# Half of the last block's input stage in two seven-product units

## The chip, the cores and the metric

The kernel runs on one core of a Trainium2 chip. Its time is the device time of one execution in microseconds (us). A profile of one execution gives a span, from the first to the last instruction, and the start and duration of nearly every instruction on the engines: PE (TensorE matmuls; PEld is its weight load), DVE (VectorE), ACT (ScalarE), POOL (GpSimd) and SP, which issues most DMAs. The engines work through their own queues in order and wait for each other with semaphores.

## The reference

Attention inside chunks of 64 tokens, then a feed-forward layer with a squared ReLU:

```python
B, H, S, D = q.shape                       # 8, 8, 576, 64
q_c, k_c, v_c = (t.reshape(B, H, S // 64, 64, D) for t in (q, k, v))
attn = softmax(q_c @ k_c^T / sqrt(D))      # per chunk, 64 x 64
x = (attn @ v_c) -> [4608 tokens, 512]     # heads side by side
h = np.maximum(x @ w_in, 0.0)              # w_in 512 x 2048
out = (h * h) @ w_out                      # w_out 2048 x 512, float32
```

## The kernel before

The 4608 tokens are cut into 18 groups of 256, two groups to a block, so there are nine blocks of 512 tokens, numbered 0 to 8. The matmul operands are bf16, sums are fp32 in PSUM. Each block j has two phases, and while they run the kernel places the attention of block j+1 and the loads, casts and transposes of block j+2 between their steps. The place is written out by hand: a counter `slot` rises by one with each step (`yield`) of a phase, and `plan` says which function is issued at which slot. A block's attention is `scores` (matmuls, then an exp on ACT, L385), `values` (matmuls, then a reciprocal and a multiplication by it on DVE, L408 and L409) and a transpose of x by DMA. Block 8 has nothing left to place: no block follows it.

The **input stage** (`ffn_in`) makes gT, the squared ReLU of x @ w_in, with d_ff on the partitions: 16 tiles of 128 rows by 512 tokens, in the order 8 to 15, then 0 to 7. A tile is four matmuls of 512 columns, one for each 128 rows of d_model (L480), into one of four PSUM banks of the pool `ps_ffn`; ACT takes the ReLU into an fp32 tile `rl` (L471, ring of three); DVE squares it into gT (L475), except tiles 10, 14 and 3, which ACT squares (L473).

The **output stage** (`ffn_out`) of blocks 1 to 8 multiplies gT by w_out in seven products of quarters instead of eight (the scheme of Strassen and Winograd). The quarters of gT are a11 and a12 (tokens 0 to 255, tiles 0 to 7 and 8 to 15), a21 and a22 (tokens 256 to 511). Each product is 16 matmuls of 256 columns (L533). They alternate between two accumulators, n and m; DVE makes the operands d5, d2, d1, d6 and d7 from gT (L493, into `w_st`) and combines the results, ACT copies n out twice (L580, L589). The first product needs a22, the second a11, the third d5 = a11 - a12.

In blocks 2 to 6 the q and k of the block after next are cast to bf16 on ACT (`cast_q` L333, `cast_k` L340) in the output stage. Their fp32 tiles `q_sb` and `k_sb` come from the pool `qk` with five buffers for each name. POOL casts the weights in block 0 (L165, L173) and q and k of the first groups up to block 2; after that it does nothing until it issues stores of the last block (L564, L568). PSUM holds the four banks of `ps_ffn` and two tiles of two banks in `ps_att`, used by the attention alone.

The order of instructions on each engine is the order in which the program issues them (`manual_schedule`). `add(engine, ...)` is a helper, so everything it issues has one line (L493).

Of the kernel before, what the change touches and what calls it, by code (L numbers as in the profile page):

```python
# [10 lines left out]
FP32 = mybir.dt.float32  # L11
BF16 = mybir.dt.bfloat16
AF = mybir.ActivationFunctionType
ALU = mybir.AluOpType
# [3 lines left out]
def kernel(  # L18
# [9 lines left out]
    nc = tc.nc  # L28

    B, H, S, D = q.shape  # L30
# [27 lines left out]
    const_pool = ctx.enter_context(tc.tile_pool(name="const", bufs=1))  # L58
    w_pool = ctx.enter_context(tc.tile_pool(name="w", bufs=1))
    wst_pool = ctx.enter_context(tc.tile_pool(name="wst", bufs=5))  # L60
    in_pool = ctx.enter_context(tc.tile_pool(name="qk", bufs=5))
    att_pool = ctx.enter_context(tc.tile_pool(name="att", bufs=3))
    ffn_pool = ctx.enter_context(tc.tile_pool(name="ffn", bufs=1))
    ps_ffn = ctx.enter_context(tc.tile_pool(name="ps_ffn", bufs=4, space=bass.MemoryType.PSUM))
    ps_att = ctx.enter_context(tc.tile_pool(name="ps_att", bufs=2, space=bass.MemoryType.PSUM))

    ctx.enter_context(tc.manual_schedule())

# [18 lines left out]
    qk = {}  # L87
# [299 lines left out]
    def values(g, tiles=(0, 1)):  # L387
        e = state["e", g]
        veb = v_even[g % NV].bitcast(BF16)
        vob = [v_odd[odd_tile[g, c] % NO].bitcast(BF16) for c in range(4)]  # L390
        if 0 in tiles:
            state["x", g] = att_pool.tile([128, 2, n_hp, 2, D], BF16, name="x", bufs=3)
        x = state["x", g]
        for t in tiles:
            ps = ps_att.tile([128, 2, 512], FP32, name="ps_att")
            for hp in range(n_hp):
                for a in range(2):
                    for p in range(2):
                        c = p ^ a
                        vb = vob[2 * t + p] if a else veb[:, t]  # L400
                        nc.tensor.matmul(  # L401
                            out=ps[64 * p:64 * p + 64, a, hp * (D + 1):(hp + 1) * (D + 1)],
                            lhsT=e[64 * c:64 * c + 64, a, hp, t, :],
                            rhs=vb[64 * c:64 * c + 64, hp, 1::2],
                            start=True, stop=True)
            o = ps[:, :, 0:n_hp * (D + 1)].rearrange("p a (h d) -> p a h d", d=D + 1)
            rec = att_pool.tile([128, 2, n_hp], FP32, name="rec", bufs=4)
            nc.vector.reciprocal(out=rec, in_=o[:, :, :, D])  # L408
            nc.vector.tensor_tensor(  # L409
                out=x[:, t].rearrange("p h a d -> p a h d"),  # L410
                in0=o[:, :, :, 0:D],
                in1=rec.to_broadcast([128, 2, n_hp, D]),
                op=ALU.mult)
# [21 lines left out]
    C, CQ, CK, TD = cast_qk, cast_q, cast_k, transpose_qk_dma  # L435
    SC, AV, XT = scores, values, transpose_x

    def TA(g):
        transpose_qk(g, ps_att, ps_att)

# [8 lines left out]

    gTs = {}  # L450
    LATE_STORES = {j: 26 if j == 2 else 20 for j in range(2, len(blocks) - 1)}
    late = []
    FT_ORDER = [*range(n_ft // 2, n_ft), *range(n_ft // 2)]

    def ffn_in(j, parts, begun={}):
        if j not in gTs:
            gTs[j] = ffn_pool.tile([128, n_ft, BT], BF16, name="gT")
        gT, xT = gTs[j], xTs[j]
        for u, (c, n, ft) in enumerate((c, n, ft) for c, n, fts in parts for ft in fts):
            h = begun.get(ft)  # L460
            if h is None:
                h = ps_ffn.tile([128, 512], FP32, name="ps_ffn")
            for dt in range(n_dt // 2 if ft in begun else 0, n_dt):
                ffn_in_step(h, xT, c, n, ft, dt)
            if j < 3:
                if n == 512 or u % 2 == 0:
                    rl_tile = ffn_pool.tile([128, 512], FP32, name="rl", bufs=3).bitcast(BF16)
                rl = rl_tile[:, u % 2 * 512:] if n < 512 else rl_tile
            else:
                rl = ffn_pool.tile([128, 512], FP32, name="rl", bufs=3)  # L470
            nc.scalar.activation(out=rl[:, 0:n], in_=h[:, 0:n], func=AF.Relu)  # L471
            if (n == 512 and ft in SQUARES_ON_ACT) or (n < 512 and ft in (12, 3)):
                nc.scalar.activation(out=gT[:, ft, c:c + n], in_=rl[:, 0:n], func=AF.Square)  # L473
            else:
                nc.vector.tensor_tensor(  # L475
                    out=gT[:, ft, c:c + n], in0=rl[:, 0:n], in1=rl[:, 0:n], op=ALU.mult)
            yield
# [14 lines left out]
    def add(engine, out, in0, in1, op=ALU.add):  # L492
        engine.tensor_tensor(out=out, in0=in0, in1=in1, op=op)  # L493
# [4 lines left out]
    def ffn_out(j):  # L498
# [110 lines left out]
        for ps, cols, t in parts("m"):  # L609
            add(nc.vector, c22[:, cols], ps, s[:, cols])  # L610
            store(nc.gpsimd, c22, 1, HD, t)
        yield from product("n", d7, b21_p_b22, False)
        c11 = o_tile()
        for ps, cols, t in parts("n"):
# [96 lines left out]
    for j, grps in enumerate(blocks):  # L711
        nxt = blocks[j + 1] if j + 1 < len(blocks) else []
        far = blocks[j + 2] if j + 2 < len(blocks) else []
        plan = {}

        def at(slot, f, g):
            plan.setdefault(slot, []).append((f, g))

        if j == 0:
            loads, go_slots = pieces(far), range(17)  # L720
            at(28, sum_quarters(b11_p_b21, b11, b21), None)
            for slot, f in ((24, TA), (27, SC), (29, AV), (31, XT)):
                at(slot, f, nxt[0])
            at(31, TQ, nxt[1])
            at(31, TK, nxt[1])
            at(31, sum_quarters(b11_m_b22, b11, b22, ALU.subtract), None)
            phases = [first_ffn_in, ffn_out_by_ft(0)]
        elif j == 1:
            loads, go_slots = itertools.chain(*map(qk_pieces, far)), range(26, 48)
            for slot, f in ((4, SC), (8, AV), (12, XT)):  # L730
                at(slot, f, grps[1])
            for i, g in enumerate(nxt):
                for slot, f in ((16 + 4 * i, C), (21 + 4 * i, TD), (36 + i, SC), (38 + 2 * i, AV),
                                (41 + 2 * i, XT)):
                    at(slot, f, g)
            for i, g in enumerate(far):
                at(36 + 4 * i, C, g)
                at(42 + 3 * i, TD, g)
            at(2, sum_quarters(b11_p_b12, b11, b12), None)
            at(12, sum_quarters(b12_p_b22, b12, b22), None)  # L740
            at(20, sum_quarters(b21_p_b22, b21, b22), None)
            phases = [ffn_in(1, [(0, 256, FT_ORDER), (256, 256, FT_ORDER)]), ffn_out(1)]
        else:
            loads, go_slots = pieces(far), range(32)
            slots = {SC: (4, 4), AV: (7, 11), XT: (10, 14), C: (18, 22), TD: (20, 24)}
            if j == 3:
                slots.update({SC: (8, 8), AV: (10, 14), XT: (13, 17)})
                go_slots = [*range(6), *range(13, 32)]
            if not is_whole(nxt[0] if nxt else 0):
                slots.update({SC: (7, 7), AV: (9, 13), XT: (12, 16)})  # L750
            if j == 2:
                loads = itertools.chain(*map(v_pieces, nxt), loads)
                slots = {SC: (8, 10), AV: (12, 15), XT: (15, 18), C: (20, 23), TD: (22, 25)}
                go_slots = [*range(16), *range(25, 36)]
            for f in (SC, AV, XT):
                for i, g in enumerate(nxt):
                    at(slots[f][i], f, g)
            if j > 2 and far and is_whole(far[0]):
                for slot, f, i in ((16, CQ, 0), (18, CK, 0), (18, TD, 0), (18, CQ, 1),
                                   (19, CK, 1), (19, TD, 1)):  # L760
                    at(slot, f, far[i])
            else:
                for f in (C, TD):
                    for i, g in enumerate(far):
                        at(slots[f][i], f, g)
            phases = [ffn_in(j, [(0, BT, FT_ORDER)]), ffn_out(j)]
        slot = 0
        for phase in phases:
            for _ in phase:
                if slot in go_slots:  # L770
                    for f in loads:
                        f()
                        break
                for f, g in plan.get(slot, []):
                    f(g)
                while late and slot >= LATE_STORES[j]:
                    late.pop(0)()
                slot += 1
        assert all(x < slot for x in plan), (j, slot, sorted(plan))
        go(loads)  # L780
        while late:
            late.pop(0)()
# [30 lines left out]
```

## Time and profile before

| | us |
|---|---|
| median of 3 runs | 283.25 |
| the runs | 285.18, 283.25, 282.54 |
| the profiled execution, its own time | 281.17 |
| its span | 279.4 |
| granted TensorE clock over the span | 0.997 |
| PE busy / DVE / ACT / POOL | 269.2 / 186.5 / 160.5 / 35.8 |
| block 8, input stage (from 249.84 to 263.65) | 13.81 |
| block 8, output stage, its 112 matmuls | 12.24 |

Times in the views count from the start of the span. A row of the groups has the line, the engine, the operation, output and inputs with their tile names, the shapes, the count, and then the busy time in us, the mean of one instruction in ns, and the idle time ahead of them with what ended it. The chain of waits is the work that ended last, followed back from the last instruction: start, length and line of each piece. A row of the timeline has start, length, engine, line and operation, with neighbours of one kind merged ("x2").

### The profile page before, as it was taken

The page shows a single profiled execution, that of the slowest core. Times are in us where ns is not written, and L with a number is a line of the kernel's source. Part 1 is how long each engine was busy: PE and PEld are TensorE (multiplying, and loading weights), DVE is VectorE, ACT ScalarE, POOL GpSimd, SP SyncE. Part 2 cuts the span into 40 slices and gives each one's busy share as a digit, 9 for nine tenths or more (in the row PEclk, how much of TensorE's full clock was granted, in tenths as well). Part 3 has the DMA queues.
Part 4 walks back from the last instruction along what each step waited for, and adds up shares of the span by engine and source line. Part 5 has one row for each costly group of instructions (what it writes and reads, how often), then busy time and mean ns, then how long its engine had stood idle before and what let it go on. Part 6 is the DMA issues. An engine that isn't in the chain of part 4 may idle for free.

```text
span 279.4 us, 7179 instructions
## 1 busy us (share of the span) xinstructions
PE 269.2 (96%) x2960; PEld 176.2 (63%) x2963; DVE 186.5 (67%) x304; ACT 160.5 (57%) x269; POOL 35.8 (13%) x62
## 2 busy tenths in 40 slices
PE   6789999989999999999999999999999999999994
PEld 4544455878774487448744874487448744874584
DVE  1446414998943595579549954995579649955793
ACT  2537615885348862877197719762877197218710
POOL 2037844240171000000000000000000000000012
PEclk9999999999999999999999999999999999999998
DMA  7999999989999999979999999979699964141003
GB/s 236 220 345 358 364 332 240 326 212 194 255 207 244 238 213 191 258 183 198 218 245 260 187 184 298 191 158 185 196 238 208 212 199 40 39 109 44 0 21 131
DMA packets 144384, 57.09 MB, mean 204 GB/s; under 512 B 110624, under 2 KB 141600, under 8 KB 144352
## 3 DMA queue, kind: packets, MB, share of 16 engines
q1 hardware_dynamic: 143296, 53.62, 83.8%
q0 software_dynamic: 912, 2.88, 2.8%
q8 instruction: 23, 0.38, 0.6%
q10 hardware_dynamic: 144, 0.13, 0.1%
q14 instruction: 9, 0.07, 0.1%
HBM read 36.70 MB, written 9.44 MB: 165 GB/s over the span
## 4 chain that ended last, share of the span: by engine, by line
PE 80%; DVE 6%; SPq 4%; ACT 2%; DMA 2%; issue 2%; POOL 0%; DVEq 0%; ACTq 0%
PE ps_ffn L480 39%; PE ps_ffn L533 32%; PE ps_ffn L626 5%; SPq L236 3%; DMA w_st<-in_moe_w_in_dram 2%; DVE x L409 2%; DVE gT L475 2%; DVE w_st L493 2%; ACT rl L471 2%; PE ps_att L401 2%; PE ps_att L374 1%; ACT e L385 1%; SPq L227 1%; PE ps_att L428 1%; PE ps_att L190 1%
## 5 line engine op out<-in xcount | busy, mean ns | idle before, releaser
L480 PE MATMUL ps_ffn<-xT,w_in_bf 128*128 128x512 bf16 (+1 forms) x640 | 130.0, 358 | 0.7 <-POOL w_in_bf L165 0.7
L475 DVE TENSOR_TENSOR gT<-rl 128x512 bf16<-128x512 f32 (+2 forms) x132 | 74.2, 593 | 61.4 <-ACT rl L471 60.7
L471 ACT ACTIVATE rl<-ps_ffn 128x512 f32<-128x512 f32 (+2 forms) x160 | 85.7, 554 | 26.9 <-PE ps_ffn L480 23.3
L480 PEld LDWEIGHTS <-w_in_bf 128*128 128x128 bf16 x640 | 60.5, 98 | 58.2 <-POOL w_in_bf L165 2.2
L533 PEld LDWEIGHTS <-w_st 128*128 128x128 bf16 x640 | 62.0, 98 | 8.2 <-DVE w_st L493 0.9
L493 DVE TENSOR_TENSOR w_st<-gT 128x2048 bf16<-128x2048 bf16 x40 | 47.3, 1217 | 0.2
L533 PE MATMUL ps_ffn<-w_out_bf,w_st 128*128 128x256 bf16 x384 | 45.1, 273 | 0.1
L533 PE MATMUL ps_ffn<-w_sum,w_st 128*128 128x256 bf16 x256 | 29.6, 273 | 0.0
L616 ACT COPY o_sb<-ps_ffn 128x512 f32<-128x512 f32 (+1 forms) x8 | 4.5, 559 | 40.3 <-PE ps_ffn L533 40.3
L533 PEld LDWEIGHTS <-gT 128*128 128x128 bf16 x256 | 24.8, 98 | 4.4 <-DVE gT L475 0.2
L568 POOL DMA_DIRECT2D out_dram<-o_sb x4 | 2.2, 553 | 186.2 <-DVE o_sb L493 186.2
L409 DVE TENSOR_TENSOR x<-ps_att,rec 128x512 bf16<-128x512 f32 x32 | 22.1, 691 | 1.1
L385 ACT ACTIVATE e<-ps_att 128x1024 bf16<-128x1024 f32 x16 | 15.8, 1022 | 4.8 <-PE ps_att L374 4.8
L473 ACT ACTIVATE gT<-rl 128x512 bf16<-128x512 f32 (+2 forms) x28 | 16.8, 599 | 0.9
L533 PE MATMUL ps_ffn<-w_out_bf,gT 128*128 128x256 bf16 x128 | 15.3, 273 | 0.0
L533 PE MATMUL ps_ffn<-w_sum,gT 128*128 128x256 bf16 x128 | 15.3, 273 | 0.0
L626 PE MATMUL ps_ffn<-w_out_bf,gT 128*128 128x512 bf16 x61 | 14.2, 379 | 0.3 <-issue 0.2
L165 POOL CAST w_in_bf<-w_st 128x1024 bf16<-128x1024 f32 (+1 forms) x9 | 9.0, 1001 | 17.9 <-DMA w_st<-in_moe_w_in_dram 17.9
L340 ACT CAST qkb<-k_sb 128x1024 bf16<-128x1024 f32 x10 | 10.5, 1047 | 1.2 <-DMA k_sb<-in_k_dram 1.2
L333 ACT CAST qkb<-q_sb 128x1024 bf16<-128x1024 f32 x10 | 10.4, 1044 | 0.0
L626 PEld LDWEIGHTS <-gT 128*128 128x128 bf16 x64 | 6.0, 98 | 7.0
L401 PEld LDWEIGHTS <-e 64*64 64x64 bf16 x512 | 5.8, 107 | 6.3 <-DVE x L409 2.1
(63 smaller groups left out, 157.1 us busy)
## 6 DMA issues: line engine op xcount, KB each, us to landing
q_sb<-in_q_dram SPq DMA_DIRECT2D x16, 512.0 KB, 6.2
k_sb<-in_k_dram SPq DMA_DIRECT2D x24, 256.0 KB, 5.8
out_dram<-o_sb SPq DMA_DIRECT2D x20, 256.0 KB, 3.7
w_st<-in_moe_w_in_dram SPq DMA_DIRECT2D x8, 512.0 KB, 6.8
w_st<-in_moe_w_out_dram SPq DMA_DIRECT2D x8, 512.0 KB, 6.1
ve_sb<-in_v_dram SPq DMA_DIRECT2D x28, 128.0 KB, 3.5
vo_sb<-in_v_dram SPq DMA_DIRECT2D x21, 128.0 KB, 3.0
out_dram<-o_sb POOLq DMA_DIRECT2D x9, 256.0 KB, 5.5
```

The costliest lines, as they stand in the source:

```text
L333: copy(out=qkb[:, 0].rearrange("p (i h d) -> p i h d", i=2, h=H), in_=qk[g][0].rearrange("p t h d -> p (t h d)").rearrange("p (h i d) -> p ...
L340: copy(out=state["qkb", g][:, 1], in_=qk[g][1].rearrange("p t h d -> p (t h d)"))
L385: nc.scalar.activation(out=e_out, in_=s_in, func=AF.Exp, scale=scale)
L401: nc.tensor.matmul(out=ps[64 * p:64 * p + 64, a, hp * (D + 1):(hp + 1) * (D + 1)], lhsT=e[64 * c:64 * c + 64, a, hp, t, :], rhs=vb[64 * c: ...
L409: nc.vector.tensor_tensor(out=x[:, t].rearrange("p h a d -> p a h d"), in0=o[:, :, :, 0:D], in1=rec.to_broadcast([128, 2, n_hp, D]), op=AL ...
L471: nc.scalar.activation(out=rl[:, 0:n], in_=h[:, 0:n], func=AF.Relu)
L473: nc.scalar.activation(out=gT[:, ft, c:c + n], in_=rl[:, 0:n], func=AF.Square)
L475: nc.vector.tensor_tensor(out=gT[:, ft, c:c + n], in0=rl[:, 0:n], in1=rl[:, 0:n], op=ALU.mult)
L480: nc.tensor.matmul(out=h[:, 0:n], lhsT=w_in_bf[:, dt, ft * 128:(ft + 1) * 128], rhs=xT[:, c // 128:(c + n) // 128, dt, :], start=(dt == 0) ...
L493: engine.tensor_tensor(out=out, in0=in0, in1=in1, op=op)
L533: nc.tensor.matmul(out=outs[t], lhsT=a[:, i, t * 128:(t + 1) * 128], rhs=b[:, i, :], start=(first and i == 0 and (last or t == 0)), stop=( ...
L626: nc.tensor.matmul(out=o_ps[tt], lhsT=gT[:, ft, tt * 128:(tt + 1) * 128], rhs=w_out_bf[:, ft, :], start=(ft == 0), stop=(ft == n_ft - 1))
```

## The change

It concerns block 8. Of its 16 input tiles, 12 to 15 (unit a) and 4 to 7 (unit b) are made by seven products of quarters each, the same scheme as in the output stage: a quarter is 256 rows of d_ff by 256 of d_model on the weights' side, and 256 of d_model by 256 tokens on the side of x. A product is four matmuls of 256 columns. The other eight tiles are made as before.

For it, POOL makes five differences of weight quarters for each unit, each of 128x512 bf16, in tiles of the pool `qk` (issued at slot 0 of blocks 6 and 7); DVE makes three sums or differences of x in block 7's output stage, behind the sixth product (`x_sums`); the PSUM of `ps_att` is given to four single banks `ps_unit`, two for each unit. ACT copies n out twice in each unit; DVE makes w, c21, s and c22 from PSUM, and POOL makes c12 from the two copies in SBUF. c21, c12 and c22 are turned into gT by one fused DVE operation, max(x, 0) * x (`scalar_tensor_tensor`, one for each, issued some steps later from the list `later`); c11 goes through a ReLU on ACT and a square on POOL. Of the eight plain tiles ACT squares 9, 11, 0 and 3, and POOL squares 8, 10, 1 and 2; DVE squares none. The order of the steps is 8, 9, a, 10, a, 11, a, b, a, 0, b, a, b, a, 1, b, a, b, 2, b, b, 3. The pool `qk` has four buffers instead of five, the ring `rl` five instead of three, both for the whole kernel. The attention's functions get a new slot only in blocks that are named in `UNITS` and have a block behind them; block 8 has none.

```diff
-    in_pool = ctx.enter_context(tc.tile_pool(name="qk", bufs=5))
+    in_pool = ctx.enter_context(tc.tile_pool(name="qk", bufs=4))
...
-    ps_att = ctx.enter_context(tc.tile_pool(name="ps_att", bufs=2, space=bass.MemoryType.PSUM))
+    ps_att, ps_unit = psum_pool("ps_att", 2), None
...
+    UNITS = {8: (12, 4)}
...
+    def quarter(f0, i, kk):
+        c = (f0 + 2 * i) * 128
+        return w_in_bf[:, 2 * kk:2 * kk + 2, c:c + 256]
+
+    def w_differences(f0, out):
+        pairs = (((0, 0), (0, 1)), ((1, 1), (1, 0)), ((0, 0), (1, 1)), ((1, 0), (0, 0)),
+                 ((0, 1), (1, 1)))
+        difs[f0] = out
+        for d, (x, y) in zip(out, pairs):
+            add(nc.gpsimd, d, quarter(f0, *x), quarter(f0, *y), ALU.subtract)
...
+    def x_sums(j):
...
+        add(nc.vector, by_dt, xT[:, :, 0:2], xT[:, :, 2:4])
+        add(nc.vector, cross, xT[:, 0:2, 0:2], xT[:, 2:4, 2:4], ALU.subtract)
+        add(nc.vector, by_t, xT[:, 0:2], xT[:, 2:4])
+        return by_dt, by_t, cross
+
+    def unit(j, f0, n, m, kept, later):
...
+        def product(out, a, b, first):
+            for f in range(2):
+                for d in range(2):
+                    nc.tensor.matmul(
+                        out=out[:, 256 * f:256 * f + 256],
+                        lhsT=a[:, d, 128 * f:128 * f + 128],
+                        rhs=b[:, :, d, :],
+                        start=(first and f == 0 and d == 0), stop=(d == 1),
+                        skip_group_check=True)
...
+        def relu_squared(x, i, jj):
+            later.append(lambda: nc.vector.scalar_tensor_tensor(
+                out=place_of(i, jj), in0=both(x), scalar=0.0, in1=both(x),
+                op0=ALU.max, op1=ALU.mult))
+
+        product(n, quarter(f0, 1, 1), by_dt[:, 0:2], True)
+        n1 = kept("n1")
+        nc.scalar.copy(out=n1, in_=n)
+        yield
+        product(m, quarter(f0, 0, 0), by_dt[:, 2:4], True)
+        w = kept("nm")
+        add(nc.vector, w, m, n1)
+        yield
+        product(n, dif[0], xT[:, 2:4, 2:4], False)
+        n2 = kept("n2")
+        nc.scalar.copy(out=n2, in_=n)
+        yield
+        product(m, dif[1], xT[:, 0:2, 0:2], False)
+        c21 = rl_tile_fp32()
+        add(nc.vector, c21, w, m, ALU.subtract)
+        c12 = rl_tile_fp32()
+        add(nc.gpsimd, c12, w, n2, ALU.subtract)
+        relu_squared(c21, 1, 0)
+        relu_squared(c12, 0, 1)
+        yield
+        product(n, dif[2], cross, False)
+        s = kept("n1")
+        add(nc.vector, s, n, n2, ALU.subtract)
+        yield
+        product(m, dif[3], by_t[:, :, 0:2], False)
+        c22 = rl_tile_fp32()
+        add(nc.vector, c22, m, s)
+        relu_squared(c22, 1, 1)
+        yield
+        product(n, dif[4], by_t[:, :, 2:4], False)
+        c11 = rl_tile_fp32()
+        nc.scalar.activation(out=c11, in_=n, func=AF.Relu)
+        add(nc.gpsimd, place_of(0, 0), both(c11), both(c11), ALU.mult)
+        yield
...
+                 2: (8, 9, "a", 10, "a", 11, "a", "b", "a", 0, "b", "a", "b", "a", 1, "b", "a", "b",
+                     2, "b", "b", 3)}
...
+                 2: {9: "A", 11: "A", 0: "A", 3: "A", 8: "P", 10: "P", 1: "P", 2: "P"}}
+    LATER = {1: (5, 10, 13, 15), 2: (9, 12, 14, 16, 18, 21)}
...
+                if by == "A":
+                    nc.scalar.activation(out=gT[:, ft], in_=rl, func=AF.Square)
+                elif by == "P":
+                    add(nc.gpsimd, gT[:, ft], rl, rl, ALU.mult)
...
+            if i in LATER[len(units)]:
+                later.pop(0)()
+            yield
...
-                rl = ffn_pool.tile([128, 512], FP32, name="rl", bufs=3)
+                rl = rl_tile_fp32()
...
+        if j + 1 in UNITS:
+            state["x_sums"] = x_sums(j + 1)
         yield from product("n", d7, b21_p_b22, False)
...
+            if j in (6, 7):
+                at(0, w_differences_in_qk, UNITS[8][j - 6])
+            if j == 8:
+                att_psum.close()
+                ps_unit = psum_pool("ps_unit", 4)
...
+            phases = [ffn_in_units(j) if j in UNITS else ffn_in(j, [(0, BT, FT_ORDER)]),
+                      ffn_out(j)]
```

## The prediction

> **What bounds the kernel now.** I read the chain of waits first, from its end.
>
> ```profile
> 237.61 12.23 PE ps_ffn L533 x112
> 249.84 13.81 PE ps_ffn L480 x64
> 263.65 12.24 PE ps_ffn L533 x112
> 275.89 0.02 issue
> 275.92 0.42 DVE o_sb L616
> ```
>
> From 237.61 to 275.89 the end hangs on PE alone, without a pause. So block 8's input stage costs what its matmuls cost: 13.81 / 64 = 0.216 us for 512 columns, and a 256-column one costs 12.24 / 112 = 0.109. Whatever leaves PE is gained, unless another engine becomes late. The stretches by engine show who has room:
>
> ```profile
> 249.84:263.65 13.81, 13.81 (x67) 6.30 (x65) 7.47 (x12) 10.98 (x19) 0.00 (x0) 1.00 0.19 45
> ```
>
> PE is full, DVE has 7.5 us of work, ACT 11.0, POOL none, and the clock is full. Then the prices, from the groups kept apart by shape:
>
> ```profile
> L471 ACT ACTIVATE rl<-ps_ffn 128x512 f32<-128x512 f32 x96 | 56.0, 597 | 17.3 <-PE ps_ffn L480 14.7 <-DVE gT L475 1.9 <-DVE rec L408 0.3
> L475 DVE TENSOR_TENSOR gT<-rl 128x512 bf16<-128x512 f32 x78 | 51.2, 687 | 41.6 <-ACT rl L471 41.1
> L493 DVE TENSOR_TENSOR nm<-ps_ffn,n 128x512 f32<-128x512 f32 x7 | 4.8, 684 | 0.6 <-PE ps_ffn L533 0.6
> L340 POOL CAST qkb<-k_sb 128x1024 bf16<-128x1024 f32 x4 | 4.3, 1078 | 5.5 <-DMA k_sb<-in_k_dram 5.5
> L165 POOL CAST w_in_bf<-w_st 128x512 bf16<-128x512 f32 x2 | 1.2, 613 | 14.7 <-DMA w_st<-in_moe_w_in_dram 14.7
> ```
>
> The change puts POOL to work beside DVE, so last I looked at the timeline where both worked, in narrow windows, DVE's answer and then POOL's:
>
> ```profile
> 61.01 0.28 DVE L475 TENSOR_TENSOR gT<-rl 128x256 bf16<-128x256 bf16 x1
> ```
> ```profile
> 59.96 1.12 DVE L475 TENSOR_TENSOR gT<-rl 128x256 bf16<-128x256 bf16 x1
> ```
> ```profile
> 59.89 1.05 POOL L333 CAST qkb<-q_sb 128x1024 bf16<-128x1024 f32 x1 [1.73 <-DMA q_sb<-in_q_dram]
> ```
> ```profile
> 78.48 0.68 DVE L493 TENSOR_TENSOR o_sb<-nm,n 128x512 f32<-128x512 f32 x1
> ```
> ```profile
> 78.75 1.31 POOL L333 CAST qkb<-q_sb 128x1024 bf16<-128x1024 f32 x1 [0.39 <-DMA q_sb<-in_q_dram]
> ```
> ```profile
> 74.16 0.69 DVE L409 TENSOR_TENSOR x<-ps_att,rec 128x512 bf16<-128x512 f32 x1
> ```
> ```profile
> 74.14 1.04 POOL L333 CAST qkb<-q_sb 128x1024 bf16<-128x1024 f32 x1 [11.35 <-DMA q_sb<-in_q_dram]
> ```
>
> The square that takes 0.28 alone took 1.12 when it started 0.07 behind a POOL cast; it ended 0.14 after the cast's end (60.94, 61.08). The other way round, the cast of 78.75 took 1.31 instead of 1.04, as DVE was on two SBUF inputs until 79.16: it ended 0.90 = 1.04 - 0.14 after that. But at 74.16 DVE, with one input in PSUM, took its usual 0.69 beside a cast. So a DVE operation on two SBUF operands and a POOL operation shut each other out, and the later one ends its own time less 0.14 after the earlier one's end; DVE with a PSUM operand goes on.
>
> **The change part by part.** PE: 32 matmuls of 512 columns become 56 of 256: 32 x 0.216 - 56 x 0.109 = 6.91 - 6.12 = 0.78 us less, if nothing makes PE wait. From the stage's start the steps would end at: a4 5.64, b2 6.94, a5 7.38, a6 8.25, tile 1 9.11, b4 9.55, b5 10.42, tile 2 11.29, b6 11.72, b7 12.16, tile 3 13.02.
>
> ACT: 8 ReLUs, 4 squares, 4 copies and 2 ReLUs of c11, 18 x 0.6 = 10.8, as now. n2 of unit a is out at 6.2, before a5 needs it; ACT holds nobody up.
>
> POOL: eight operations of 128x512 fp32 with two inputs, which no row shows. The nearest is the 1024-element cast, which reads as many elements: 1.05. Lower end 0.61, the 512-element cast; upper end 1.3, the longest cast there is. I take 1.05. [...]
>
> DVE: its 13 squares go. In their place are 14 operations: in each unit w, c21, s and c22 with a PSUM operand (0.69 each) and three fused squares on two SBUF operands. The fused form is in no row; nearest is the square on the same operands and types, 0.69; ends 0.43 (the bf16 square) and 1.22 (L493 on 2048 elements). I take 0.69. A next independent operation starts 0.61 after the one before, one on its result 0.71. In the order of issue: c21a 5.74 to 6.43. POOL took up c12a at 6.28 (to 7.33), so the square of c21a ends 7.33 + 0.55 = 7.88 instead of 7.14. w_b 7.80 to 8.49, s_a 8.41 to 9.10, square c12a to 9.71, c22a 9.63 to 10.32. The square of c22a meets POOL's square of tile 1 (ReLU out at 9.81; POOL 9.89 to 10.94) and ends 11.49. c21b, ready since 9.65, runs 11.41 to 12.10. **PE wants to start b6, which adds to the bank that c21b reads, at 11.29 and starts at 12.16: 0.87 lost.** POOL's c12b waits for DVE and ends 12.40; the square of c21b ends 12.95; s_b runs 12.87 to 13.56. **b7 could start at 12.60 and starts at 13.62: 1.02 lost.** The stage takes 13.02 + 0.87 + 1.02 = 14.91 instead of 13.81: **+1.1**.
>
> Behind it: POOL's last square (c11b) ends at 16.8. The second product reaches that tile at 14.92 + 1.75 + 0.44 = 17.1, and d5 (DVE, 16.8 to 18.0) is wanted at 18.4. Both are in time by 0.3, so 0. With POOL at 1.3 the same walk gives 15.4 for the stage, and the second product waits 0.45: +2.1. With 0.61 it gives +1.0. With no shutting out only b7 waits, 0.55, as DVE's chain c21b, square, s_b ends at 12.22: -0.2. The fused square at 0.43 gives +0.2, at 1.22 +3.7. [...]
>
> The weight differences on POOL wait only for their buffers, and POOL has been idle since 85 us. Unit a's buffer is free when ACT has cast q of group 13, at 157.01 + 1.05 = 158.06, unit b's at 187.33 + 1.05 = 188.38, so they run in the output stages of blocks 4 and 5 and shut DVE's d1, d6, d7 out.
>
> ```profile
> 158.12 2.35 DVE L493 TENSOR_TENSOR w_st<-gT 128x2048 bf16<-128x2048 bf16 x2
> 160.82 0.69 DVE L493 TENSOR_TENSOR o_sb<-nm,ps_ffn 128x512 f32<-128x512 f32 x1 [0.34 <-PE ps_ffn L533]
> 161.42 1.22 DVE L493 TENSOR_TENSOR w_st<-gT 128x2048 bf16<-128x2048 bf16 x1
> ```
>
> If d1 (158.12) starts first, d6 ends at 161.3 and d7 at 163.3; the products want them at 162.5 and 164.3: no wait. If POOL is first, each is a POOL operation later, c21 ends 0.3 late and s again 0.3: +0.6. They start within 0.1 of each other; DVE's is queued and POOL's must see ACT's signal, so I take +0.1. In block 5, d6 is done at 188.48 and d7 has 1.5 us to spare: 0.
>
> Costed at nothing: `x_sums` (two of 1024 and one of 512 bf16 elements, at most 0.69 + 0.42 + 0.69 by the copies and squares of these sizes) falls into DVE's 2.61 us of idle time ahead of 251.43; if that cover is gone, a1 is late from 251.57 on. The PSUM banks were last used in block 7's attention. Four buffers in `qk`: SP's order of issue is unchanged, and a buffer comes back two blocks after its cast. The longer `rl` ring frees ACT from waits on DVE, 1.9 us in the row above, but PE does not hang on them: 0, at best -0.2.
>
> Sum: 1.1 + 0.1 = +1.2 on the profiled execution, 281.17 (span 279.4 and 1.77 around it), so 282.4. The median shown is 283.25, 2.1 above that execution; on it, **284.5**.
>
> **The rivals.** [...] (B) POOL is the bound: at 1.3 or more its last three squares run back to back and the second product and d5 wait for c11b: +2.1 and more, 285.4 to 286. For it: POOL reads two operands; against it: the cast's row. (C) The weight differences stall blocks 4 or 5: +0.6 in place of +0.1, 285.0. (D) The change does nothing to the bound: excluded, since PE is full and its work falls; only the sign is open.
>
> **How the numbers follow.** Forecast (+0.4 to +1.8) 0.55; A 0.2; B 0.13; C 0.07; others 0.05. The range takes in A's full gain, 282.5, and B with C, 286.0; its ends are rounded to 282.4 and 286.0. The forecast's own range is 283.6 to 285.1. One per cent is 2.8 us, about what a measurement tells from no change. A can't reach that: faster 0.02. Slower needs more than B with C, or a fused square near its far end (1.22: +3.7, 287): 0.08. Same 0.90.
>
> **What would show it.** In block 8's input stage: PE idle ahead of b6 and b7, waiting for DVE (c21b, s_b); fused squares of over 1 us where POOL is busy, 0.69 elsewhere; POOL's operations near 1.05. In the chain the stretch before the last 112 matmuls would be 14.9 long, with DVE pieces in it. POOL's ten differences would stand at 158 to 166 and 188 to 195. I am wrong if the stage takes under 13.3, if fused squares beside POOL take 0.69, or if PE waits for POOL at the second product.

## The result and the profile after

| | before | after |
|---|---|---|
| median, us | 281.66 (22 runs) | 285.04 (22 runs) |
| lowest to highest, us | 280.85 to 285.18 | 282.77 to 286.97 |
| profiled execution, its own time / span, us | 281.17 / 279.4 | 284.55 / 282.8 |
| granted TensorE clock over the span | 0.997 | 0.994 |
| block 8, first input matmul to start of last copy, us | 26.08 | 29.13 |
| its input stage / 112 output matmuls, us | 13.81 / 12.24 | 16.46 / 12.65 |

The ratio of after to before is 1.0105, 95% interval [1.0082, 1.0127]: the changed kernel is slower by about 3 us. In the changed kernel's lines L643 is the input matmul, L514 the matmul of a unit, L696 that of the output stage, L656 the helper `add`, L528 the fused square, L602 and L605 ReLU and square on ACT.

The end of the chain of waits, changed kernel (start, length, work):

```profile
254.59 1.32 PE ps_unit L514 x12
255.91 0.02 issue
255.94 0.70 DVE rl L656
256.63 0.02 issue
256.66 0.59 DVE gT L528
...
261.67 0.61 DVE rl L656
262.28 0.02 issue
262.31 0.04 DVE gT L528
262.34 0.93 issue
263.28 0.69 DVE q_sb L656
263.96 0.04 issue
264.01 1.01 PE ps_unit L514 x4
265.02 1.71 PE ps_ffn L643 x4
266.72 12.65 PE ps_ffn L696 x112
```

Where before had one unbroken piece of PE, 13.81 long, the chain now leaves PE at 255.91 and runs through DVE until 263.96: c21a, its fused square, then c21b (261.67) and s_b (263.28). The "issue" of 0.93 is s_b waiting for the fused square that started at 262.31. PE's timeline has the two places where it paid:

```profile
262.32 0.60 PE L514 MATMUL ps_unit<-w_st,q_sb 128*128 128x256 bf16 x4 [0.78 <-DVE rl L656]
264.01 1.01 PE L514 MATMUL ps_unit<-w_st,k_sb 128*128 128x256 bf16 x4 [1.09 <-DVE q_sb L656]
```

These are b6 and b7. With a matmul's run-in after each pause (0.16: the four matmuls of b6 take 0.60, and in an unbroken row the next four start 0.44 after), PE stood 0.94 and 1.25, together 2.19 us. But b7 took 1.01 instead of 0.60, and the next tile 1.71 instead of 0.86. The stretches by engine, in four equal pieces, say why (length, PE busy, PEld, DVE, ACT, POOL, granted clock, DMA share, GB/s):

```profile
257.19:260.60 3.41, 3.41 (x30) 2.67 (x28) 3.41 (x5) 2.34 (x5) 1.09 (x2) 1.00 0.00 0
260.60:264.01 3.41, 1.54 (x10) 0.69 (x9) 3.34 (x6) 0.88 (x2) 3.41 (x3) 1.00 0.00 0
264.01:267.42 3.41, 3.41 (x13) 1.77 (x13) 2.20 (x3) 1.23 (x3) 3.05 (x3) 0.50 0.02 5
267.42:270.83 3.41, 3.41 (x33) 3.06 (x32) 2.71 (x4) 1.34 (x3) 0.00 (x0) 1.00 0.00 0
```

PE was busy for 1.54 of 3.41 us while it waited for b6 and b7, and in the next 3.41 us its clock was half. That halved stretch cost 0.41 (b7) + 0.85 (the tile) + 0.41 (12.65 instead of 12.24) = 1.67 us. So block 8 comes out: -0.79 (smaller matmuls) + 2.19 (waits) + 1.67 (clock) = +3.07, against 29.13 - 26.08 = 3.05 measured.

DVE's fused squares and POOL's operations on either side of them, from the timelines of the two engines:

```profile
256.66 1.66 DVE L528 SCALAR_TENSOR_TENSOR gT<-rl 128x512 bf16<-128x512 f32 x1
...
259.44 0.68 DVE L528 SCALAR_TENSOR_TENSOR gT<-rl 128x512 bf16<-128x512 f32 x1
...
262.31 1.05 DVE L528 SCALAR_TENSOR_TENSOR gT<-rl 128x512 bf16<-128x512 f32 x1
```
```profile
254.39 1.04 POOL L656 TENSOR_TENSOR gT<-rl 128x512 bf16<-128x512 f32 x1 [1.46 <-ACT rl L602]
256.49 1.27 POOL L656 TENSOR_TENSOR rl<-nm,n 128x512 f32<-128x512 f32 x1 [1.06 <-ACT n L542]
...
261.08 1.72 POOL L656 TENSOR_TENSOR rl<-q_sb,k_sb 128x512 f32<-128x512 f32 x1
```

A fused square alone takes 0.68; the one that started 0.17 behind POOL's c12a took 1.66 and ended at 258.32, 0.56 after c12a's end (257.76), which is its own time less 0.12. A POOL square, with one tile as both inputs, takes 1.04 alone; c12, which reads two tiles, takes 1.27 (256.49), though only operations with a PSUM operand and the square it holds up stand beside it.

The second place is block 4's output stage, where PE had no pause before. The changed kernel's timelines of PE, DVE and POOL there:

```profile
162.56 1.91 PE L696 MATMUL ps_ffn<-w_sum,w_st 128*128 128x256 bf16 x16 [0.59 <-DVE o_sb L656]
164.66 1.03 PE L696 MATMUL ps_ffn<-w_out_bf,w_st 128*128 128x256 bf16 x8 [0.19 <-DVE n L656]
```
```profile
157.20 0.68 DVE L656 TENSOR_TENSOR nm<-ps_ffn,n 128x512 f32<-128x512 f32 x1
157.80 2.02 DVE L656 TENSOR_TENSOR w_st<-gT 128x2048 bf16<-128x2048 bf16 x1
```
```profile
157.59 1.15 POOL L656 TENSOR_TENSOR q_sb<-w_in_bf 128x512 bf16<-128x512 bf16 x1 [72.72 <-DMA vo_sb<-in_v_dram]
```

POOL's first weight difference was 0.21 ahead of DVE's d1, d1 took 2.02 instead of 1.22, and c21 and s came late; with the run-in PE lost 0.75 and 0.35, together 1.1 us. The group of unit a's and b's differences in `q_sb` has a mean of 1700 ns, where one alone takes 1.15 us:

```profile
L656 POOL TENSOR_TENSOR q_sb<-w_in_bf 128x512 bf16<-128x512 bf16 x8 | 13.4, 1700 | 95.2 <-DMA vo_sb<-in_v_dram 72.7
```

### The profile page after: what moved, and what is told of

It reads as the page before. It is cut to its first block, busy times and chain, and to the rows that moved or that the text cites. A ratio compares the mean times of both kernels' runs of the same rounds, so it can differ in the third digit from the quotient of the medians.

```text
span 282.8 us, 7242 instructions
## 1 busy us (share of the span) xinstructions
PE 270.4 (96%) x2987; PEld 179.2 (63%) x2987; DVE 193.4 (68%) x308; ACT 160.4 (57%) x268; POOL 62.8 (22%) x80
## 5 line engine op out<-in xcount | busy, mean ns | idle before, releaser
L643 PE MATMUL ps_ffn<-xT,w_in_bf 128*128 128x512 bf16 (+1 forms) x608 | 124.7, 359 | 0.7 <-ACT rl L634 0.7
L638 DVE TENSOR_TENSOR gT<-rl 128x512 bf16<-128x512 f32 (+2 forms) x119 | 65.6, 583 | 52.0 <-ACT rl L634 51.1
L643 PEld LDWEIGHTS <-w_in_bf 128*128 128x128 bf16 x608 | 57.6, 98 | 53.3 <-POOL w_in_bf L171 1.8
L634 ACT ACTIVATE rl<-ps_ffn 128x512 f32<-128x512 f32 (+2 forms) x144 | 76.3, 550 | 23.4 <-PE ps_ffn L643 22.0
L696 PEld LDWEIGHTS <-w_st 128*128 128x128 bf16 x640 | 61.9, 98 | 9.2 <-DVE w_st L656 1.1
L656 DVE TENSOR_TENSOR w_st<-gT 128x2048 bf16<-128x2048 bf16 x40 | 49.8, 1280 | 2.1 <-ACT gT L605 1.9
L696 PE MATMUL ps_ffn<-w_out_bf,w_st 128*128 128x256 bf16 x384 | 45.1, 273 | 0.3 <-DVE n L656 0.2
L656 POOL TENSOR_TENSOR q_sb<-w_in_bf 128x512 bf16<-128x512 bf16 x8 | 13.4, 1700 | 95.2 <-DMA vo_sb<-in_v_dram 72.7
L696 PE MATMUL ps_ffn<-w_sum,w_st 128*128 128x256 bf16 x256 | 29.8, 273 | 0.6 <-DVE o_sb L656 0.6
L696 PEld LDWEIGHTS <-gT 128*128 128x128 bf16 x256 | 25.2, 99 | 4.8 <-issue 0.6
L656 POOL TENSOR_TENSOR gT<-rl 128x512 bf16<-128x512 f32 x6 | 7.4, 1244 | 59.7 <-ACT rl L602 59.6
L696 PE MATMUL ps_ffn<-w_sum,gT 128*128 128x256 bf16 x128 | 15.7, 277 | 0.0
L636 ACT ACTIVATE gT<-rl 128x512 bf16<-128x512 f32 (+2 forms) x25 | 14.9, 595 | 0.8
L696 PE MATMUL ps_ffn<-w_out_bf,gT 128*128 128x256 bf16 x128 | 15.3, 272 | 0.0
```

What stands on the lines that cost most here:

```text
L638: nc.vector.tensor_tensor(out=gT[:, ft, c:c + n], in0=rl[:, 0:n], in1=rl[:, 0:n], op=ALU.mult)
L643: nc.tensor.matmul(out=h[:, 0:n], lhsT=w_in_bf[:, dt, ft * 128:(ft + 1) * 128], rhs=xT[:, c // 128:(c + n) // 128, dt, :], start=(dt == 0) ...
L696: nc.tensor.matmul(out=outs[t], lhsT=a[:, i, t * 128:(t + 1) * 128], rhs=b[:, i, :], start=(first and i == 0 and (last or t == 0)), stop=( ...
```

## The experiments

The theory from the profile after: DVE and POOL shut each other out on SBUF operands (the fused square of 0.68 took 1.66), so b6 and b7 wait (2.19 us); these waits halve the clock where they fall badly (1.67); the weight differences stop block 4 (1.1). The rivals: POOL is simply too slow; the waits have nothing to do with the shutting out; the clock halves at random; the smaller pool costs time in the earlier blocks. All diffs are against the changed kernel unless said otherwise. "Block 8" is from its first input matmul to the start of its last copy, read from each kernel's chain.

### The weight differences left out

```diff
-            add(nc.gpsimd, d, quarter(f0, *x), quarter(f0, *y), ALU.subtract)
+            pass
+        difs[f0] = [quarter(f0, *x) for x, _ in pairs]
```

> The changed kernel without the ten weight differences on GpSimd: the products of the units read a plain quarter of the weights in their place, so part of the computation is left out; matmuls, their shapes and everything in block 8 stay. Theory (two-operand work on GpSimd and VectorE shuts each other out, and the five differences for unit a cost block 4's output stage its 1.1 us): that output stage is back at 12.2 us from 13.3, and the time is 1.1 under the changed kernel, about 283.9 or a ratio to before of 1.007. Rival (block 4's two pauses, 0.75 and 0.36, come from the smaller buffer pools or are chance): the pauses stay and the ratio stays at 1.0105.

Measured: 283.19 us, ratio 1.0067 [1.0038, 1.0096]. Block 4's output stage has no pause; block 8 is 29.13, as in the changed kernel, halved clock included. The differences cost about 1.1 us (1.0105 less 1.0067; the two intervals overlap), and the stage says where: block 4's pauses, 0.75 and 0.35, are gone, and block 8 has not changed.

### The squares issued later

```diff
-    LATER = {1: (5, 10, 13, 15), 2: (9, 12, 14, 16, 18, 21)}
+    LATER = {1: (5, 10, 13, 15), 2: (9, 12, 17, 19, 20, 21)}
```

> Only the place of the fused squares in VectorE's queue is changed: those of c22a, of c21b and of c12b are issued behind s_b and c22b instead of between c21b and s_b. Theory (b6 and b7 wait because squares that GpSimd shuts out stand ahead of c21b and s_b): both waits go (2.0 us), TensorE's clock stays full (1.8 us), and GpSimd's queue becomes the next bound: the second product of the output stage waits about 1 us for c11b. Block 8's input stage takes 13.0 to 13.4, the time falls by 2.5 to 3, to a ratio of 1.000 to 1.003. Rival (VectorE's work in the block is too much in any order, or the pause is TensorE's own): the stage stays above 15 and the ratio at 1.0105.

Measured: 284.2 us, ratio 1.0102 [1.0064, 1.0139]. The waits of b6 and b7 went (0 and 0.14), and two others came in the output stage:

```profile
267.42 1.64 PE L696 MATMUL ps_ffn<-w_out_bf,gT 128*128 128x256 bf16 x13 [0.65 <-ACT gT L605]
269.86 1.38 PE L696 MATMUL ps_ffn<-w_out_bf,w_st 128*128 128x256 bf16 x11 [0.80 <-DVE w_st L656]
```

With the run-in these are 0.82 and 0.97. PE's second product and d5 now wait for squares that are made too late. The first wait is put down to ACT, but it ends as DVE's second fused square of a row of three does (267.41), and the chain runs through POOL's square, c12b and square (1.04, 1.23 and 1.46 from 261.36 on) and the DVE squares behind them. Block 8 is 27.27. The forecast of the ratio failed: the wait was moved more than removed, so 27.27 is still 1.2 above before, and block 4's 1.1 stayed.

### Memsets in POOL's place

POOL's eight operations of block 8 become memsets of the same tiles, so those squares and c12 are not computed.

```diff
-        add(nc.gpsimd, c12, w, n2, ALU.subtract)
+        nc.gpsimd.memset(c12, 1.0)
...
-        add(nc.gpsimd, place_of(0, 0), both(c11), both(c11), ALU.mult)
+        nc.gpsimd.memset(place_of(0, 0), 1.0)
...
-                    add(nc.gpsimd, gT[:, ft], rl, rl, ALU.mult)
+                    nc.gpsimd.memset(gT[:, ft], 1.0)
```

> GpSimd's eight operations in block 8 are replaced by memsets on the same outputs: they write as much but read nothing, so the squares and c12 are left out. Theory (the shutting out is between two operations that both read two or one operands in SBUF through what they share): the fused squares take 0.69 each, b6 does not wait, b7 waits 0.55 at most, the clock stays full, the stage takes 13.0 to 13.6 and the ratio falls to 1.000 to 1.003, what block 4 costs. Rival 1 (VectorE's fused square is slow by itself, or the chain c21b, square, s_b too long): b6 and b7 wait as before, 2 us, ratio 1.0105. Rival 2 (GpSimd blocks VectorE whatever it does): fused squares beside a memset are as long as the memset allows, and part of the waits stay.

Measured: 282.04 us, ratio 1.0035 [1.0011, 1.0058]; block 8 26.05, input stage 13.79. POOL writes as many tiles, but reads nothing, and every fused square falls to 0.69, the one beside a memset too (timelines of DVE, then of POOL):

```profile
258.25 0.68 DVE L528 SCALAR_TENSOR_TENSOR gT<-rl 128x512 bf16<-128x512 f32 x1
```
```profile
258.23 0.52 POOL L564 MEMSET gT<- 128x512 bf16 x1
```

b6 does not wait, b7 waits 0.60 (0.77 with the run-in): near what the prediction gave for no shutting out, 0.55. So POOL's operations that read SBUF held the fused square up here (1.66 beside c12a), memsets of the same tiles did not (0.68 beside one of 0.52), and this is the cause of the waits. (The ratio is 1.0 us above what block 8 alone gives. Runs with block 4's pauses would explain it, but the one profile has none, so that stays open.) This profile held a second answer by chance. Block 4's output stage had no pause in it, and POOL's first difference was there 0.07 behind d1 instead of ahead of it (DVE, then POOL):

```profile
158.24 1.22 DVE L656 TENSOR_TENSOR w_st<-gT 128x2048 bf16<-128x2048 bf16 x1
```
```profile
158.31 2.16 POOL L656 TENSOR_TENSOR q_sb<-w_in_bf 128x512 bf16<-128x512 bf16 x1 [73.31 <-ACT qkb L339]
```

### PE kept busy through the waits

8 and 9 matmuls of 256 columns, into a bank that unit a has done with, fill the pauses ahead of b6 and b7; their results go nowhere.

```diff
+            for _ in range({19: 8, 20: 9}.get(i, 0)):
+                nc.tensor.matmul(out=m_a[:, 0:256], lhsT=ident, rhs=ident_f32.bitcast(BF16),
+                                 start=True, stop=True)
             if ft in todo:
                 next(todo[ft])
```

> The changed kernel with 8 and 9 idle matmuls of 256 columns (0.87 and 0.98 us) on TensorE ahead of b6 and of b7, where it waited 0.8 and 1.2 us; nothing else is changed. Theory (the clock was halved from 263.7 to 267.1 because TensorE had paused for 2 us in 3): TensorE is busy through both waits, the clock stays at 1.00, tile 3 takes 0.86 instead of 1.71 and the stage 14.9 instead of 16.5; the time falls by about 1.8 although work is added, ratio 1.004. Rival (the half clock comes from something else, the power of the moment or the end of the program): the half clock stays and the ratio is 1.0105 or a little more.

Measured: 283.47 us, ratio 1.008 [1.0049, 1.0111]. The stage keeps its full clock, and b7 its 0.60:

```profile
251.36:266.56 15.20, 15.10 (x107) 10.30 (x106) 10.60 (x15) 9.72 (x17) 8.73 (x7) 1.00 0.18 43
```

Block 8 is 27.46, 1.67 less than in the changed kernel, with 17 matmuls more. The ratio fell less than forecast, for a reason that the records of all runs gave later: the clock is halved in block 8 in some executions only (an estimated quarter, from the mean clocks of 57 runs below).

### The two pool settings alone

Diff against the kernel before:

```diff
-    in_pool = ctx.enter_context(tc.tile_pool(name="qk", bufs=5))
+    in_pool = ctx.enter_context(tc.tile_pool(name="qk", bufs=4))
...
-                rl = ffn_pool.tile([128, 512], FP32, name="rl", bufs=3)
+                rl = ffn_pool.tile([128, 512], FP32, name="rl", bufs=5)
```

> The kernel before with two of the changed kernel's settings alone: four q and k buffers instead of five, and five rl buffers instead of three; no units. Theory (the prediction's 0): ratio 0.998 to 1.002 against the kernel before, block 8's input stage 13.8 us. Rival: the earlier blocks lose time to the smaller pool, since q and k are loaded later; then the ratio lies at 1.003 or above, and a part of the changed kernel's +3 us is lost ahead of block 8.

> The kernel before with four q and k buffers and five rl buffers alone, again. Theory: ratio 0.999 to 1.001. Rival (the longer rl ring is a gain of its own): ratio 0.996 to 0.998, as the kernel with all.

Measured: 281.0 us, ratio 0.9975 [0.9943, 1.0007], and in a second set 281.76 us, 0.9988 [0.9955, 1.0022]. Block 8 is 26.08 both times. No cost of the settings shows (the upper ends are 0.07% and 0.22%); a small gain is not excluded.

### The differences moved behind c21, in blocks 5 and 6

```diff
-            if j in (6, 7):
-                at(0, w_differences_in_qk, UNITS[8][j - 6])
...
             store(nc.gpsimd, c21, 1, 0, t)
+        if j in (5, 6):
+            hold = ffn_pool.tile([128, 16], BF16, name="hold", bufs=1)
+            nc.gpsimd.tensor_copy(out=hold, in_=c21[:, 0:16])
+            w_differences_in_qk(UNITS[8][j - 5])
```

> The changed kernel with only the weight differences moved, to behind c21 in the output stages of blocks 5 and 6. Theory (block 4's pauses come from POOL's differences, which shut DVE's d1, d6 and d7 out there): block 4 has no pause, block 8 is as in the changed kernel (input stage 16.4 us with waits of 0.8 and 1.2 us and the halved clock), ratio 1.006 to 1.009 against the kernel before, as without the differences (1.0067). Rival (they cost wherever they stand): as the changed kernel, 1.0105 or more, with pauses in block 5 or 6.

Measured: 283.47 us, ratio 1.0068 [1.0032, 1.0104], as without the differences (1.0067). Block 4's output stage has no pause; block 6's has one of 0.25, which ends at 217.03, ahead of POOL's first operation there (217.88), so it is not theirs. This profile also shows the waits without the halved clock (timeline of PE):

```profile
263.27 0.60 PE L514 MATMUL ps_unit<-w_st,q_sb 128*128 128x256 bf16 x4 [0.78 <-DVE rl L656]
264.95 0.60 PE L514 MATMUL ps_unit<-w_st,k_sb 128*128 128x256 bf16 x4 [1.08 <-DVE q_sb L656]
265.38 1.03 PE L643 MATMUL ps_ffn<-xT,w_in_bf 128*128 128x512 bf16 x4
```

The same waits as in the changed kernel, yet b7 and the tile run at full speed: the input stage is 251.21 to 266.41, 15.20, and block 8 27.46, exactly 1.67 below the changed kernel's profile.

### The differences behind d1, in blocks 4 and 5

As the last one, but at `d1` and with `j in (4, 5)`:

```diff
         d1 = difference(a11, a22)
+        if j in (4, 5):
+            hold = ffn_pool.tile([128, 16], BF16, name="hold", bufs=1)
+            nc.gpsimd.tensor_copy(out=hold, in_=d1[:, 0, 0:16])
+            w_differences_in_qk(UNITS[8][j - 4])
```

> The changed kernel with POOL's weight differences issued behind d1 in the output stages of blocks 4 and 5 (a 16-column copy of d1 on POOL makes it wait for that), so that DVE is first there. Theory (who is first decides: in the profile with memsets in block 8 the first difference happened to start 0.07 us behind d1, and block 4 had no pause, where it started 0.2 ahead the pauses were 1.1 us): no pause in block 4, block 8 as in the changed kernel, ratio 1.006 to 1.009 against the kernel before. Rival (the differences cost wherever they overlap d6 and d7): pauses of 0.5 us or more remain in block 4 or 5, ratio 1.009 to 1.012.

Measured: 283.84 us, ratio 1.0058 [1.0026, 1.0091]; no pause in the output stages of blocks 4 and 5, block 8 27.46. The differences overlap d7 in the same block and cost PE nothing. Part of that is the copy itself: it started at 160.42, 0.15 behind d6, was shut out by it, and ended at 161.54, just after d6 (161.49), so the first difference began only at 161.50. The kernel shows that a start behind d1 and d6 is free, and the profile with memsets that a start just behind d1 is.

### Longer waits

As the kernel with the differences moved behind c21, and for unit b two DVE operations twice:

```diff
         add(nc.vector, c21, w, m, ALU.subtract)
+        if f0 == 4:
+            add(nc.vector, c21, w, m, ALU.subtract)
...
         add(nc.vector, s, n, n2, ALU.subtract)
+        if f0 == 4:
+            add(nc.vector, s, n, n2, ALU.subtract)
```

> The kernel with only the differences moved (ratio 1.0068), with c21b and s_b each computed twice on DVE: two operations of 0.69 us more in the chain that b6 and b7 wait for. The waits grow from 0.8 and 1.2 us to about 1.5 and 1.8. Theory (idle time of PE inside a stretch of 3.41 us halves the clock of the next one; with longer pauses nearly every position of the stretches catches enough of it): the clock is below 0.995 in nearly every run, instead of in about half of them, and the time grows by the waits, 1.2 to 1.4 us, and by half or more of a halved stretch, 0.9 us: ratio 1.013 to 1.018. Rival (the halved clock comes at random and has nothing to do with the waits): the clock as often below 0.995 as before, and only the waits are added: ratio 1.010 to 1.012.

Measured: 287.76 us, ratio 1.0187 [1.0138, 1.0235]. The waits grew to 1.50 and 2.09, the second more than expected, and the clock halved after them (stretches by engine):

```profile
261.20:264.60 3.40, 2.20 (x17) 1.44 (x15) 3.33 (x6) 1.79 (x3) 2.66 (x2) 1.00 0.00 0
264.60:268.00 3.40, 1.01 (x8) 0.76 (x8) 3.33 (x5) 0.00 (x0) 2.50 (x3) 1.00 0.00 0
...
268.10:271.40 3.30, 3.30 (x14) 1.68 (x13) 1.47 (x4) 1.82 (x3) 1.41 (x1) 0.50 0.02 5
```

A stretch with PE busy for 2.20 of 3.40 us was not followed by a halved one, a stretch with 1.01 was.

For why the same waits halve the clock in one run and not in another there is an estimate, from the edges of the clock. In the changed kernel's profile the halved stretch lasts 3.413 us (264.01 to 267.42), and the clock falls again at 284.49, 17.07 us after it rose: five times 3.413. In the profile of the kernel with the differences behind d1 it fell at 14.84, rose at 18.25 and fell again at 281.08, behind the last matmul: the two later edges are 262.83 us apart, 77 times 3.413. If the stretches follow each other at that length between these edges too, which no row shows, one ends in this run at 264.01, in b7's wait, so that no stretch holds both waits (stretches by engine):

```profile
260.60:264.01 3.41, 2.29 (x16) 1.37 (x15) 3.34 (x5) 1.35 (x3) 3.18 (x3) 1.00 0.00 0
264.01:267.42 3.41, 2.67 (x21) 2.01 (x21) 2.94 (x5) 1.74 (x4) 3.41 (x3) 1.00 0.02 5
```

PE is busy for 2.29 and 2.67 of 3.41 us, and the clock stays full; in the changed kernel's profile both waits fell into one stretch, 1.54 of 3.41.

The record of every run has its mean clock, and one halved stretch of 3.41 us in 282 makes it 0.994. It was below 0.995 in 6 of 6 runs here; in 33 of 57 runs of the four kernels with waits of 0.8 and 1.1 us (the changed one, without differences, both moved ones); in 27 of 85 runs of the kernel before and 19 of 75 of the other kernels without two such waits (the lower clock need not lie in block 8: the profile of the kernel with the differences behind d1 has a mean of 0.993 with block 8 at full clock, the half clock lying at 14.84 to 18.25 and behind the last matmul). So the waits of 0.8 and 1.1 us halve the clock in an estimated quarter of the runs (33/57 - 27/85 = 0.26, with a 95% interval of some 0.1 to 0.4), and with the longer ones the mean was below 0.995 in all six.

### Less for POOL and later squares, without and with the moved differences

```diff
-    LATER = {1: (5, 10, 13, 15), 2: (9, 12, 14, 16, 18, 21)}
+    LATER = {1: (5, 10, 13, 15), 2: (9, 12, 17, 19, 20, 21)}
...
-                 2: {9: "A", 11: "A", 0: "A", 3: "A", 8: "P", 10: "P", 1: "P", 2: "P"}}
+                 2: {9: "A", 11: "A", 0: "A", 3: "A", 8: "P", 10: "A", 1: "A", 2: "P"}}
...
-        add(nc.gpsimd, place_of(0, 0), both(c11), both(c11), ALU.mult)
+        nc.scalar.activation(out=place_of(0, 0), in_=both(c11), func=AF.Square)
```

> The changed kernel with less for POOL and later squares on DVE: tiles 10 and 1 and c11 are squared on ACT, tiles 8 and 2 stay with POOL, and the fused squares of c22 and of unit b are issued behind c21b and s_b. Theory (the waits of b6 and b7 come from fused squares that POOL shuts out, and the waits halve the clock): no wait ahead of b6 and b7, none ahead of the second product and the third, full clock; input stage 13.0 to 13.2 us, block 8 from its first input matmul to its last copy out 25.3 to 25.7 us, against 26.08 before and 29.13 with the change. The pauses of about 1.1 us in block 4 stay, so the ratio against the kernel before is 0.999 to 1.003. Rival (the units themselves are slow, for example through ACT's two copies of n, which then compete with four more ACT squares): PE waits for ACT inside the input stage, which stays above 14 us, and the ratio is 1.004 or more.

Measured: 281.06 us, ratio 0.9997 [0.9965, 1.0029]. The input stage has no wait and lasts what its matmuls cost, 13.02; block 8 is 25.29, 0.79 below before. Block 4's pauses (0.75 and 0.35) are there.

With the differences also moved behind c21 in blocks 5 and 6:

> As the kernel with less for POOL and later squares, and the weight differences moved: POOL makes them behind c21 in the output stages of blocks 5 and 6 (a 16-column copy of c21 on POOL makes it wait for that), where DVE has less to do. Theory: block 8 as in that kernel (25.3 to 25.7 us), no pause in block 4, ratio 0.996 to 0.999 against the kernel before: what the 56 smaller matmuls save, 0.78 us, is then left over. Rival (the differences cost wherever they stand, since they shut DVE out there too): a pause of 0.5 us or more in block 5 or 6 in place of block 4's, ratio 1.000 to 1.003.

> The kernel with less for POOL, later squares and the differences moved, again, beside the kernel before with the two pool settings alone, to see whether it beats both kernels and whether the units do it. Theory: ratio 0.996 to 0.998 (0.78 us less on PE), and 0.78 us below the kernel with the pool settings alone. Rival (the gain is that of the pool settings): no difference between the two.

Measured: 280.18 us, ratio 0.9959 [0.9925, 0.9994], and again 282.02 us, 0.9973 [0.9937, 1.001]. Block 8 is 25.29 both times, and the chain is PE alone to the end:

```profile
262.86 0.87 PE ps_unit L514 x8
263.73 0.86 PE ps_ffn L643 x4
264.59 12.24 PE ps_ffn L696 x112
```

b6 and b7 (the x8) follow on the tile before them without a pause. By the ratios this version is faster than the changed kernel by 3.7 to 4.1 us and lies 0.8 to 1.2 us below the kernel before, with the second interval reaching just past 1. That it is the units that do it is shown for block 8, not for the whole time: the kernel with the pool settings alone ran in the same two sets at 0.9975 and 0.9988, and the intervals overlap. The 0.78 us below that kernel that was expected was not measured: by the ratios it is 0.4, and in the second set the medians are the other way round (282.02 against 281.76).

## Why the prediction was right, and where it was not

The time, 285.04, is near the 284.5 predicted, but the change is not: +1.2 was predicted, +3.0 came (1.05% of 281.66), outside the forecast's +0.4 to +1.8. That the two times nearly agree is luck: 284.5 was made on the median of three runs, 283.25, and 22 runs have theirs at 281.66. Made on that, it would have been 282.9.

| step | predicted, us | measured, us |
|---|---|---|
| PE's matmuls in block 8 | -0.78 | -0.79 (13.02 in the kernel with less for POOL) |
| b6 waits | 0.87 | 0.78, with run-in 0.94 |
| b7 waits | 1.02 | 1.09, with run-in 1.25 |
| input stage without a halved clock | 14.91 | 15.20 |
| POOL, 128x512 fp32, two inputs | 1.05 | 1.04 (squares), 1.27 (c12, two tiles) |
| fused square alone | 0.69 | 0.68 |
| second product, d5 | 0 | 0 |
| differences, block 4 | 0.1 | 1.1, where POOL is first |
| differences, block 5 | 0 | 0 |
| pool settings | 0 | -0.25% and -0.12%, neither clear of noise |
| clock | full, 0 | 1.67 in an estimated quarter of the runs, 0.4 in the mean |

Summed, -0.79 + 2.19 + 1.1 + 0.4 = 2.9, against the 3.0 of the ratio. Without the differences, or with them moved, 1.8 is left, against 1.9, 1.9 and 1.6 by the three ratios.

**The walk through block 8 was right**, step for step, but for two sizes: c12 takes 1.27 and not 1.05, and each wait has a run-in of 0.16 that the sum left out. It had c21b from 11.41 to 12.10 and s_b from 12.87 to 13.56 after the stage's start; they ran from 11.34 and 13.02. What it walked by came from three pairs of rows of the kernel before, and that it holds for the fused square too, which is in no row there, was the author's assumption. The changed kernel's 1.66 shows it, and the memsets do from the other side: take POOL's reads away, and b7 waits 0.60, b6 not at all, with a memset of 0.52 beside a fused square of 0.68. Rival A (the shutting out does not bite, and up to PE's 0.78 is gained) and rival B (POOL is the bound) fell with the same rows: fused squares of up to 1.66, POOL squares of 1.04 alone, no wait at the second product. Rival B's wait can be had, as the kernel with later squares shows, 0.82 and 0.97.

**The step that failed is "the clock is full".** It was read off a stage in which PE never stopped, and then kept for a stage with 2 us of pauses. No term of the sum held what a pause does to the work behind it. The profiles give what was missing: behind a stretch of 3.41 us with two pauses of 0.94 and 1.25 (PE busy 45%) the clock was 0.50 for 3.41 us, while behind one with PE busy 65%, in the kernel with longer waits, it stayed at 1.00.

**The other step is the price of the differences in block 4**, rival C in kind. The prediction took DVE to be first, since its operation was queued. POOL was first in four of the five profiles with the differences in that place, by 0.12 to 0.22 us: in the changed kernel's, ACT's cast frees the buffer at 157.50, POOL begins at 157.59, and d1, queued behind w, at 157.80. The order DVE first costs nothing, as was said; the order POOL first costs 1.1, not 0.6, since d6 and d7 then wait for POOL operations that had themselves been waiting for DVE (2.13 us each instead of 1.15). What decides is how far DVE is behind PE: counted from the stage's first matmul, POOL starts at 4.51 to 4.52 in all five, and d1 starts at 4.45 with the memsets and at 4.64 to 4.73 in the other four. In the one profile of the kernel before it starts at 4.49 (158.12, against 153.63), so the prediction read a margin of hundredths from a run in which DVE was early.

What stays open: profiles differ ahead of block 8 in ways that do not follow the change. PE waits for the transposing DMA of x before a block's first matmul in some profiles and not in others with the same pool settings (0.89 us in one with the pool settings alone, none in the changed kernel's), so the ratios have intervals of 0.2% and more to each side, and smaller effects were read from the stages alone. Where in a run the 3.41-us stretches begin was not set in any kernel here, and how the clock goes behind a stretch with PE busy between 45% and 65% was not measured.

## What to carry to other kernels

Before work is moved to GpSimd, list for each DVE operation on the path whether it reads two SBUF operands, and walk the queue with the later of two such operations ending its own time after the earlier (here less 0.12: 1.66 instead of 0.68); work that has left DVE's queue can still hold it up from there. Price a pause on TensorE at more than its length: here two of 0.94 and 1.25 within 3.41 us were followed by half the clock for 3.41 us, which cost another 1.67. Where two engines become free within 0.2 us of each other, price both orders and fix the better one with a dependence.

## What the runs showed of the hardware

- The granted clock went to 0.50 for 3.41 us after a stretch in which PE was busy for 1.54 of 3.41 us, and in another kernel 1.01 of 3.40; the same waits in other runs left it at 1.00.
- A GpSimd `tensor_tensor` of 128x512 takes 1.04 us (fp32, one tile as both inputs), 1.27 (fp32, two tiles) and 1.15 (bf16, two tiles); when the last one and DVE's 128x2048 difference shut each other out in turn, it takes 2.13 and DVE's 2.02 to 2.17 instead of 1.22.
- A GpSimd memset of 128x512 took 0.52 beside a fused square of DVE on two SBUF operands, which took its 0.68, and 0.53 with nothing of DVE beside it: neither held the other up.
- A 16-column copy on GpSimd, issued to make it wait, took 1.12 to 1.13 us (behind d1 and behind c21). Each time it had started 0.14 to 0.16 behind a 1.22-us difference on DVE and ended 0.05 to 0.06 after it, from which the author takes the length for the shutting out; its own time was not measured.
